# One of the 32 rows of wo in each partition is loaded at the start of the kernel, on ScalarE's DMA queue

## The chip, the cores and the metric

One core of a Trainium2 chip runs the kernel. The metric is the device time in microseconds (us); less is better. The engines are PE (TensorE), DVE (VectorE), ACT (ScalarE), POOL (GpSimd) and SP (SyncE, which here only issues DMAs). DMAs are issued by SP and by ACT, each into a queue of its own, and 16 DMA engines work for both.

## The reference

One decode step. Attention of 16 query heads over 8 cached KV heads of 65,536 positions with 256 elements each, a gated ReLU feed-forward part beside it, and a mix of the two by a scalar gate:

```python
g = sigmoid((x * gate_w).sum(-1, keepdims=True))          # x: [1, 1, 448]
q = (x @ wq).reshape(B, Sq, 16, 256)                       # wq: [448, 4096]
p = softmax(einsum("bhqd,bhkd->bhqk", q, k) / 16)          # k, v: [1, 8, 65536, 256], bf16
a = einsum("bhqk,bhkd->bhqd", p, v).reshape(1, 1, 4096) @ wo   # wo: [4096, 448]
b = (relu(x @ W_gate) * (x @ W_up)) @ W_down               # 448 -> 1792 -> 448
return g * a + (1 - g) * b
```

K and V are 256 MB each and are read once; the weights are some 12 MB. Nearly all that is read is K and V.

## The kernel before, in words

K and V are cut into 32 tiles each of 8 MB (128 partitions of 64 KB), four for each KV head. Three SBUF buffers, `ring0` to `ring2`, take them: K tiles alternate between `ring1` and `ring2`, V tiles use `ring0` until the last four, and the weights use `ring0` while no V tile needs it.

Each K tile is transposed in place by DVE in four instructions (`f_trans`, L529), multiplied by the queries on PE (`f_qk`, L540), reduced to its maximum on DVE (L703) and exponentiated on ACT (L705). V tiles are multiplied on PE (L584). At the end `f_sel` (L557) turns the last head's result into `attnA`, and `f_wo` multiplies it by wo (`proj`, L551), whose 4096 rows lie as 32 rows in each of the 128 partitions. The two halves of the result go through a copy each (L796, L797) and out by one DMA.

The order of the work is written by hand: every operation has an engine and a key, a time that its author planned for it, and each engine executes its operations in the order of their keys. A class `_Plan` works out the semaphore waits. DMAs that SP issues stand in one list (`order`): K tile 0, wq (one large and one small DMA), K tile 1, W_down (`wd`), K tile 2, W_gate and W_up, K tile 3, then K and V tiles by turns, the last V tile in three pieces, and wo in chunks of whole rows (L393):

```python
WO = [(0, 11), (11, 18), (18, 23), (23, 27), (27, 30), (30, 32)]
```

A K tile is issued once the tile two places earlier has been multiplied: K tile 2 waits for the second half of K tile 0's `f_qk`. SP issues in order, so what stands behind such a wait in SP's list waits too.

ACT issues only two DMAs, both at the very start: `x` (one row of 896 bytes, into `P_sb`, L421) and `gate_w` (the same size, into `scr`, L422). What needs them stands early on DVE, ahead of the transposes of K tile 0:

- `x0_` (L478, L479) copies part of x to `xeo`, PE turns x (L485), and DVE spreads it to `xw` (L492, L494), which the projection with wq (`f_q`, L501) needs;
- `z0` to `z9` (L464 to L475, with a step on ACT at L466 and one on PE at L471) work out the gate from x and gate_w, on one partition.

Behind these on DVE come the four transposes of K tile 0 (L529), the transpose of the projected queries (L632, which waits for ACT's copy of them, L630), their spreading to `xm` (L513), and `nselT` (L636). `f_qk` of K tile 0 runs once these are through.

Of the kernel before, what the change touches and what calls it, by code (L numbers as in the profile page):

```python
# [27 lines left out]
class _Plan:  # L28
# [8 lines left out]
    def op(self, eng, key, fn, deps=(), tag=None):  # L37
        eng, cls = {"pv": ("pe", "pv"), "dx": ("dv", "dx"), "ap": ("ac", "ap")}.get(eng, (eng, eng))
        o = _Op(eng, key, fn, deps, tag=tag, cls=cls)
        self.ops.append(o)  # L40
        return o

    def dma(self, eng, key, sem, fn, deps=()):
        if sem not in self.dsem:
            self.dsem[sem] = self.es.enter_context(self.nc.semaphore("d_" + sem))
        o = _Op(eng, key, fn, deps, dma=sem)
        self.ops.append(o)
        return o
# [212 lines left out]
def bass_gated_mix__gqa_block_cached__glu_gated_reglu__decode_kernel(  # L261
# [16 lines left out]
    D = A_x.shape[2]  # L278
# [18 lines left out]
    with es:  # L297
# [4 lines left out]
        P_sb = sb("P_sb", [128, 2048], BF)  # L302
        pcur = [sb("pcur%d" % i, [128, 256], BF) for i in range(2)]
        ptp = sb("ptp", [128, 1024], BF)
        scr = sb("scr", [128, 1024], BF)
# [21 lines left out]
        attnA = sb("attnA", [128, 32], BF)  # L327
# [11 lines left out]
        x_row = P_sb[0:1, 1312:1312 + D]  # L339
        fin_o = P_sb[0:1, 0:D]  # L340
        gw_row = scr[0:1, 0:D]
        xeo = scr[0:1, 448:704]
        qrep = scr[:, 0:512]
        gtmp = ptp[0:1, 0:2 * D].bitcast(F32)

# [25 lines left out]
        op, dma = pl.op, pl.dma  # L371
# [17 lines left out]
        for i, (lo, hi) in enumerate(PIECES):  # L389
            order.append(("vp", i, TILE * (hi - lo) / U))  # L390

        WO = [(0, 11), (11, 18), (18, 23), (23, 27), (27, 30), (30, 32)]
        for i, (lo, hi) in enumerate(WO):  # L393
            order.append(("wo", i, 0.27 * (hi - lo)))
        t = 3.0
        tL, issue = {}, []
# [21 lines left out]
        wo_sb = ring[slot["wo", 0]][:, 0:32 * D].rearrange("p (s n) -> p s n", s=32)  # L418


        d_x = dma("ac", -9, "x", lambda e: e.dma_start(x_row, A_x[0, :, :]))  # L421
        d_gw = dma("ac", -8, "gw", lambda e: e.dma_start(gw_row, gate_w.rearrange("(o d) -> o d", o=1)))  # L422

# [125 lines left out]
        def proj(e, lhsT, rhs, start, stop):  # L549
            for g in range(2):  # L550
                ins = e.matmul(A_ps[32 * g:32 * g + 1, 0:D2], lhsT, rhs[:, g * D2:(g + 1) * D2], start=start, stop=stop,  # L551
                               skip_group_check=True, tile_position=(0, 32 * g))
            return ins
# [7 lines left out]
        l_, qk, smax, aexp, pv, pc, last, first = {}, {}, {}, {}, {}, {}, {}, {}  # L561
# [62 lines left out]
        for kind, i, t in sorted(issue, key=lambda q: q[0] != "wq"):  # L624
# [51 lines left out]
            elif kind == "k":  # L676
                n = i
# [30 lines left out]
                if t_ == NTH - 1:  # L708
# [18 lines left out]
                    for rd in range(2):  # L727
# [10 lines left out]
                        p = op("pe", tt + 0.5, f_ptr, [rsc, g_idb], tag=("ptr", rd))  # L738
# [29 lines left out]
            elif kind in ("v", "vp"):  # L768
                if kind == "v":
                    n, lo, hi = i, 0, U  # L770
# [12 lines left out]
            elif kind == "wo":  # L783
                lo, hi = WO[i]
                l_["wo", i] = dma("sp", t, "wo%d" % i, lambda e, lo=lo, hi=hi: e.dma_start(  # L785
                    wo_sb[:, lo:hi, :], A_wo.rearrange("(p s) n -> p s n", s=32)[:, lo:hi, :]), free(("wo", 0)))

        LAST = last["tn", H - 1]
        aA = op("dx", LAST + 0.3, lambda e: e.tensor_copy(attnA[:], AX_ps), [last["otr", H - 1]])
        for i, (lo, hi) in enumerate(WO):  # L790
            def f_wo(e, lo=lo, hi=hi):
                for s_ in range(lo, hi):
                    ins = proj(e, attnA[:, s_:s_ + 1], wo_sb[:, s_, :], False, s_ == 31)
                return ins
            fin = op("pv", max(LAST + 0.5 + i, tL["wo", i]), f_wo, [l_["wo", i], aA, l_["dn"]])
        f0 = op("dx", T_END, lambda e: e.tensor_copy(fin_o[:, 0:D2], A_ps[0:1, 0:D2]), [fin])  # L796
        f1 = op("ap", T_END, lambda e: e.copy(fin_o[:, D2:D], A_ps[32:33, 0:D2]), [fin])  # L797
        f2 = dma("sp", T_END + 1, "out", lambda e: e.dma_start(out[0, :, :], fin_o), [f0, f1])
# [77 lines left out]
```

## Time and profile before

| | |
|---|---|
| time, median of 3 runs | 1276.04 us (1276.03 to 1276.18) |
| span of the profiled execution, first to last instruction | 1274.3 us |
| bytes read | 549.03 MB, 431 GB/s over the span |
| busy: PE, DVE, ACT, POOL | 29%, 49%, 6%, 0% of the span |
| mean granted clock of TensorE | 0.634 |
| first K tile: issue to landing | 22.1 us |

The page gives no device time for the profiled execution by itself; its span lies 1.7 us under the median of the three runs, which spread over 0.15 us. "L464" is line 464 of the kernel before; in the changed kernel the same lines stand two to four lines further down. In the DMA tables q1 is the queue of the DMAs that SP issues, and q10 that of ACT's: in the whole trace it holds four packets, those of x and gate_w.

### The profile page before, as it was taken

The page shows a single profiled execution, that of the slowest core. Times are in us where ns is not written, and L with a number is a line of the kernel's source. Part 1 is how long each engine was busy: PE and PEld are TensorE (multiplying, and loading weights), DVE is VectorE, ACT ScalarE, POOL GpSimd, SP SyncE. Part 2 cuts the span into 40 slices and gives each one's busy share as a digit, 9 for nine tenths or more (in the row PEclk, how much of TensorE's full clock was granted, in tenths as well). Part 3 has the DMA queues.
Part 4 walks back from the last instruction along what each step waited for, and adds up shares of the span by engine and source line. Part 5 has one row for each costly group of instructions (what it writes and reads, how often), then busy time and mean ns, then how long its engine had stood idle before and what let it go on. Part 6 is the DMA issues. An engine that isn't in the chain of part 4 may idle for free.

```text
span 1274.3 us, 10240 instructions
## 1 busy us (share of the span) xinstructions
PE 365.9 (29%) x4497; PEld 151.4 (12%) x4505; DVE 630.1 (49%) x309; ACT 78.0 (6%) x163; POOL 4.6 (0%) x23
## 2 busy tenths in 40 slices
PE   0534321133320332312233222323302332112525
PEld 0101110011110111101111110111100111001201
DVE  4777655553455633557433565335654355553300
ACT  0001100010000100001000010000000010000100
POOL 1000000000000000000000000000000000000000
PEclk9766665666655666656666656666566666566667
DMA  9999999999999999999999999999999999999998
GB/s 411 430 436 432 426 430 434 432 443 432 430 432 432 434 442 430 430 434 430 438 438 430 430 434 430 440 438 428 430 434 430 444 434 428 430 436 430 442 421 369
DMA packets 11389, 549.13 MB, mean 431 GB/s; under 512 B 1267, under 2 KB 1654, under 8 KB 2294
## 3 DMA queue, kind: packets, MB, share of 16 engines
q1 hardware_dynamic: 11378, 549.03, 99.7%
q8 instruction: 4, 0.07, 0.0%
q14 instruction: 3, 0.02, 0.0%
q10 hardware_dynamic: 4, 0.00, 0.0%
HBM read 549.03 MB, written 0.00 MB: 431 GB/s over the span
## 4 chain that ended last, share of the span: by engine, by line
DMA 81%; PE 16%; DVE 2%; ACT 1%; issue 1%; SPq 0%; ACTq 0%
DMA ring<-in_A_v_cache_dram 74%; PE O L584 13%; DMA ring<-in_A_wo_dram 3%; DMA ring<-in_A_wq_dram 2%; DMA ring<-in_A_k_cache_dram 2%; DVE ring L529 1%; PE ST L540 1%; ACT pcur L591 1%; PE O L501 1%; PE A_ps L551 0%; SPq L785 0%; SPq L776 0%; PE O L653 0%; DVE ring L660 0%; PE A_ps L653 0%
## 5 line engine op out<-in xcount | busy, mean ns | idle before, releaser
L529 DVE STREAM_TRANSPOSE ring<-ring 128x4096 uint32<-128x4096 uint32 x128 | 557.6, 4413 | 196.9 <-DMA ring<-in_A_k_cache_dram 196.9
L584 PE MATMUL O<-ring,pcur 128*4 128x512 bf16 x2048 | 187.3, 545 | 790.4 <-ACT pcur L591 781.9
L703 DVE TENSOR_REDUCE nmb<-ST 128x1 f32<-128x512 f32 x32 | 22.1, 692 | 345.9 <-PE ST L540 345.9
L584 PEld LDWEIGHTS O<-ring,pcur 128*4 128x4 bf16 x2048 | 59.3, 111 | 914.8 <-ACT pcur L591 794.6
L540 PE MATMUL ST<-ring,xcur 128*16 128x512 bf16 x2048 | 136.7, 420 | 44.3 <-DVE ring L529 43.7
L540 PEld LDWEIGHTS ST<-ring,xcur 128*16 128x16 bf16 x2048 | 62.4, 92 | 112.1 <-DVE ring L529 48.6
L705 ACT ACTIVATE P_sb<-ST,nmb 128x512 bf16<-128x512 f32 x32 | 44.6, 1392 | 368.3 <-DVE nmb L703 368.3
L591 ACT COPY pcur<-ptp 128x256 bf16<-128x256 bf16 x32 | 13.2, 415 | 732.6 <-DMA ring<-in_A_v_cache_dram 732.6
L607 DVE TENSOR_SCALAR o_sb<-O,rcm 128x256 bf16<-128x256 f32 x8 | 3.8, 479 | 61.1 <-PE O L584 61.1
L730 DVE TENSOR_TENSOR P_sb<-P_sb,hs 128x1024 bf16<-128x1024 bf16 x16 | 18.9, 1222 | 8.1 <-ACT hs L724 8.1
L735 PE MATMUL PT<-identb,P_sb 128*128 128x128 bf16 x128 | 14.5, 282 | 17.6 <-DVE P_sb L730 17.3
L501 PE MATMUL O<-ring,P_sb 128*128 128x512 bf16 x28 | 8.5, 477 | 17.3 <-DMA ring<-in_A_wq_dram 17.3
L735 PEld LDWEIGHTS PT<-identb,P_sb 128*128 128x128 bf16 x128 | 10.7, 127 | 19.9 <-DVE P_sb L730 19.9
L744 ACT COPY ptp<-PT 128x256 bf16<-128x256 bf16 x32 | 10.3, 375 | 23.0 <-PE PT L735 23.0
L705 ACT ACTIVATION_READ_ACCUMULATOR P_sb<-ST,nmb 128x1 f32 x32 | 8.3, 258 | 0.0
L501 PEld LDWEIGHTS O<-ring,P_sb 128*128 128x128 bf16 x28 | 3.2, 117 | 22.2 <-issue 20.5
L551 PE MATMUL A_ps<-ring,attnA 128*1 128x224 bf16 x64 | 5.3, 322 | 1.1 <-DMA ring<-in_A_wo_dram 1.0
L719 PE MATMUL M_ps<-identf,hs 128*2 128x128 f32 x8 | 2.3, 283 | 10.0 <-DVE hs L717 10.0
L756 DVE RECIPROCAL rc<-M_ps 128x2 f32<-128x2 f32 x8 | 1.4, 171 | 7.5 <-PE M_ps L755 7.5
L755 PE MATMUL M_ps<-hs,ones_f 128*128 128x2 f32 x16 | 4.5, 352 | 0.0
L722 PE MATMUL M_ps<-mx,nselT 2*128 2x1 f32 x16 | 3.2, 268 | 3.0 <-DVE mx L721 3.0
L755 PEld LDWEIGHTS M_ps<-hs,ones_f 128*128 128x128 f32 x16 | 4.0, 311 | 0.0
(93 smaller groups left out, 68.6 us busy)
## 6 DMA issues: line engine op xcount, KB each, us to landing
ring<-in_A_v_cache_dram SPq DMA_DIRECT2D x1, 4096.0 KB, 22.1
ring<-in_A_wq_dram SPq DMA_DIRECT2D x1, 3072.0 KB, 28.9
ring<-in_A_v_cache_dram SPq DMA_DIRECT2D x1, 3072.0 KB, 28.8
ring<-in_B_W_down_dram SPq DMA_DIRECT2D x1, 1568.0 KB, 53.0
ring<-in_B_W_gate_dram SPq DMA_DIRECT2D x1, 1344.0 KB, 26.3
ring<-in_B_W_up_dram SPq DMA_DIRECT2D x1, 1344.0 KB, 29.2
ring<-in_A_wo_dram SPq DMA_DIRECT2D x1, 1232.0 KB, 33.0
ring<-in_A_v_cache_dram SPq DMA_DIRECT2D x1, 1024.0 KB, 30.7
```

The source lines that it names most:

```text
L501: ins = e.matmul(QN_ps, xw3[:, kt, 31 - m:159 - m], rhs, start=(kt == 0 and m == 0), stop=(kt == R3 and m == J // 4 - 1))
L529: return lambda e: e.transpose(v, v)
L540: ins = e.matmul(bank[32 * w:32 * w + 16, :], xcur[:, x0:x0 + 16], ktv[sl][:, u0:u0 + 16, c, :, r_], start=(b == 0 and c == 0 and r_ == 0) ...
L551: ins = e.matmul(A_ps[32 * g:32 * g + 1, 0:D2], lhsT, rhs[:, g * D2:(g + 1) * D2], start=start, stop=stop, skip_group_check=True, tile_pos ...
L584: ins = e.matmul(OP[32 * g:32 * g + 4, :], pcur[a % 2][:, 4 * k:4 * k + 4], ring[sl][:, k * 512:(k + 1) * 512], start=False, stop=False, s ...
L591: pc[n] = op("ap", max(tp - 5, last["tev", h] - 0.5), lambda e: e.copy(pcur[a % 2][:].rearrange("p (k i) -> p k i", i=4), ptp[:].rearrange ...
L703: smax[n] = op("dv", sx, lambda e, n=n, t_=t_: e.tensor_reduce(NM[:, t_:t_ + 1], ST[n % 2][:], AX.X, ALU.max, negate=True), [qk[n, 1], las ...
L705: aexp[n] = op("ac", sx + 1, lambda e, n=n, t_=t_: e.activation(P_sb[:, t_:2048:4], ST[n % 2][:], ACTF.Exp, bias=NM[:, t_:t_ + 1], scale=1 ...
L730: rsc = op("dv", tt, lambda e, pb=pb: e.tensor_tensor(pb, pb, X[:, 12:16].unsqueeze(1).to_broadcast([128, 256, 4]), ALU.mult), [h7, aexp[n]])
L735: ins = e.transpose(PT[rd][:, s * 128:(s + 1) * 128], P_sb[:, (rd * 8 + s) * 128:(rd * 8 + s + 1) * 128], identb[:, :])
L744: ins = e.copy(dst, src)
L755: l3 = mop("pe", T + 19, lambda e: e.matmul(LS_ps, ones_f[:, :], X[:, 6:8], start=True, stop=True), [l2, c_one], tag="l3")
```

## The change

wo's row 31 in each partition no longer comes with the last chunk. It is a DMA of its own, `d_wl`, with 128 rows of 896 bytes (0.11 MB), into a free part of `scr`, and ACT issues it as its first, ahead of x and gate_w. The last chunk of wo has one row in each partition instead of two, and ends with row 30. The product with row 31 is taken first of all 32, and waits for `d_wl` too. `xeo` moves from `scr` to `P_sb`, since `wo_l` takes its place.

```diff
-        xeo = scr[0:1, 448:704]
+        xeo = P_sb[0:1, 1776:2032]
+        wo_l = scr[:, 576:576 + D]
...
-        WO = [(0, 11), (11, 18), (18, 23), (23, 27), (27, 30), (30, 32)]
+        WO = [(0, 11), (11, 18), (18, 23), (23, 27), (27, 30), (30, 31)]
...
+        d_wl = dma("ac", -10, "wl", lambda e: e.dma_start(wo_l[:], A_wo.rearrange("(p s) n -> p s n", s=32)[:, 31, :]))
         d_x = dma("ac", -9, "x", lambda e: e.dma_start(x_row, A_x[0, :, :]))
         d_gw = dma("ac", -8, "gw", lambda e: e.dma_start(gw_row, gate_w.rearrange("(o d) -> o d", o=1)))
...
             def f_wo(e, lo=lo, hi=hi):
+                if lo == 0:
+                    proj(e, attnA[:, 31:32], wo_l[:], False, False)
                 for s_ in range(lo, hi):
-                    ins = proj(e, attnA[:, s_:s_ + 1], wo_sb[:, s_, :], False, s_ == 31)
+                    ins = proj(e, attnA[:, s_:s_ + 1], wo_sb[:, s_, :], False, s_ == 30)
                 return ins
-            fin = op("pv", max(LAST + 0.5 + i, tL["wo", i]), f_wo, [l_["wo", i], aA, l_["dn"]])
+            fin = op("pv", max(LAST + 0.5 + i, tL["wo", i]), f_wo, [l_["wo", i], aA, l_["dn"], d_wl])
```

The start of ACT's program before (`P_sb` from `in_A_x` is x, `scr` from `in_gate_w` is gate_w):

```order
L836 UNCONDITIONAL_BRANCH
L421 DMA P_sb<-in_A_x_dram 1x448
L422 DMA scr<-in_gate_w_dram 1x448
L466 ACT_TABLE_LOAD
L466 ACTIVATE gz<-gz 1x1
L630 CAST ptp<-O 128x512
L634 COPY xcur<-xm 128x136
```

The same place in the changed kernel:

```order
L840 UNCONDITIONAL_BRANCH
L422 DMA scr<-in_A_wo_dram 128x448
L423 DMA P_sb<-in_A_x_dram 1x448
L424 DMA scr<-in_gate_w_dram 1x448
L468 ACT_TABLE_LOAD
L468 ACTIVATE gz<-gz 1x1
L632 CAST ptp<-O 128x512
L636 COPY xcur<-xm 128x136
```

The new DMA stands ahead of both others; nothing else on ACT moves, and DVE's order stays as it was.

The end of PE's program before, with the semaphores that a row waits for (`d_wo1` to `d_wo5` are the landings of the chunks of wo):

```order
L551 MATMUL A_ps<-ring,attnA 1x224 [waits s_dx,d_wo0]
L551 MATMUL A_ps<-ring,attnA 1x224 x21
L551 MATMUL A_ps<-ring,attnA 1x224 [waits d_wo1]
L551 MATMUL A_ps<-ring,attnA 1x224 x13
L551 MATMUL A_ps<-ring,attnA 1x224 [waits d_wo2]
L551 MATMUL A_ps<-ring,attnA 1x224 x9
L551 MATMUL A_ps<-ring,attnA 1x224 [waits d_wo3]
L551 MATMUL A_ps<-ring,attnA 1x224 x7
L551 MATMUL A_ps<-ring,attnA 1x224 [waits d_wo4]
L551 MATMUL A_ps<-ring,attnA 1x224 x5
L551 MATMUL A_ps<-ring,attnA 1x224 [waits d_wo5]
L551 MATMUL A_ps<-ring,attnA 1x224 x3
```

And in the changed kernel, from the second matmul with row 31 (the first stands one row ahead and waits for `d_wl`, `s_dx` and `d_wo0`):

```order
L553 MATMUL A_ps<-scr,attnA 1x224
L553 MATMUL A_ps<-ring,attnA 1x224 x22
L553 MATMUL A_ps<-ring,attnA 1x224 [waits d_wo1]
L553 MATMUL A_ps<-ring,attnA 1x224 x13
L553 MATMUL A_ps<-ring,attnA 1x224 [waits d_wo2]
L553 MATMUL A_ps<-ring,attnA 1x224 x9
L553 MATMUL A_ps<-ring,attnA 1x224 [waits d_wo3]
L553 MATMUL A_ps<-ring,attnA 1x224 x7
L553 MATMUL A_ps<-ring,attnA 1x224 [waits d_wo4]
L553 MATMUL A_ps<-ring,attnA 1x224 x5
L553 MATMUL A_ps<-ring,attnA 1x224 [waits d_wo5]
L553 MATMUL A_ps<-ring,attnA 1x224
```

The two matmuls with row 31 move from behind the last wait to the first group, and behind the last wait two are left of four.

## The prediction

> **What bounds the kernel now.** I read the page first, for the share of the DMA engines, then the chain that ended last at both ends of the program, and then the start of ACT and DVE in the timeline, since that is where the change puts its new transfer. The page's DMA rows:
>
> ```profile
> DMA  9999999999999999999999999999999999999998
> DMA packets 11389, 549.13 MB, mean 431 GB/s; under 512 B 1267, under 2 KB 1654, under 8 KB 2294
> q1 hardware_dynamic: 11378, 549.03, 99.7%
> q10 hardware_dynamic: 4, 0.00, 0.0%
> ```
>
> The 16 DMA engines are busy in every slice, and SP's queue alone fills 99.7% of them. So a stretch in which they stand idle is added to the time, and bytes that only change their place take nothing off it. The reader should keep one figure from here: 431 GB/s over 16 engines is 26.9 GB/s for one, so a row of 64 KB, as each partition of a K tile has, takes one engine 65,536 / 26.9e3 = 2.43 us. A K tile is 128 rows, eight for each engine. The chain at the start and at the end:
>
> ```profile
> 1.66 29.70 DMA ring<-in_A_wq_dram
> 31.49 8.51 PE O L501 x28
> 50.70 24.64 DMA ring<-in_A_k_cache_dram
> ...
> 1236.40 35.84 DMA ring<-in_A_wo_dram
> 1272.24 0.04 issue
> 1272.28 0.38 PE A_ps L551 x4
> 1272.66 0.02 issue
> 1272.68 0.38 DVE P_sb L796
> ```
>
> K tile 2 is issued at 50.70, when K tile 0 is through, and lands at 75.34. At the end the last chunk of wo lands at 1272.24, four matmuls take 0.38, and a copy and the store follow. Everything between is transfers.
>
> **The change part by part.** At the end two things shrink. The last chunk has 0.11 MB less, which at 431 GB/s is 0.27 us of transfer, but these bytes are read at the start instead: whether that saves anything depends on whether they find idle engines there, so this term lies between -0.27 and 0, and below 0 on the bad side too by a little, since 128 rows of 1,792 bytes become 256 of 896 with an end packet more. I put it at -0.2. Behind the last wait two matmuls of four are left: at 0.38 / 4 apiece that is -0.19, but the pipeline's last result takes its time whatever stands ahead of it, so between -0.19 and 0; I take -0.1. The two matmuls moved to the first group lie beside the wait for the next chunks, and the wait for `d_wl` there comes over a millisecond after its issue: nothing. `xeo` in another tile is the same three small instructions on DVE: nothing. The tail is worth about -0.3, between -0.46 and +0.1.
>
> At the start ACT now issues 128 rows ahead of x and gate_w, while SP issues K tile 0. How the two queues shared the engines before is seen best in the packets of ACT's queue, q10. It holds four in all: two for each of its two DMAs, which I read as the row and the packet that signals its end (the table counts packets by size, and one in each pair is under 512 bytes). The DMA view over six stretches, 1.5 to 1.7, 1.7 to 7.3, 7.3 to 7.4 (both queues), 7.4 to 9.7 and 9.7 to 9.8 us:
>
> ```profile
> DMA packets 2, 0.00 MB, mean 4 GB/s; under 512 B 1, under 2 KB 2, under 8 KB 2
> q10 hardware_dynamic: 2, 0.00, 1.9%
> ...
> q1 hardware_dynamic: 33, 2.16, 101.4%
> ...
> q1 hardware_dynamic: 3, 0.20, 453.6%
> q10 hardware_dynamic: 1, 0.00, 2.6%
> ...
> q1 hardware_dynamic: 12, 0.79, 78.9%
> ...
> q1 hardware_dynamic: 4, 0.26, 604.8%
> q10 hardware_dynamic: 1, 0.00, 0.6%
> ```
>
> x goes through at 1.5 to 1.7, just before K tile 0's first row starts. gate_w does not: it waits until 7.3, while 33 K rows start on the 16 engines (two on each, and a third on one), and then its end packet waits until 9.7, one K row of 2.43 us more. So an engine that has K rows waiting serves ACT's queue by turns: one K row, one packet of ACT, one K row. The issues and the first users of these two DMAs, from the timelines of ACT's and SP's queue and of DVE:
>
> ```profile
> 0.72 0.52 ACTq L421 DMA_DIRECT2D P_sb<-in_A_x_dram  x1
> 1.27 0.21 ACTq L422 DMA_DIRECT2D scr<-in_gate_w_dram  x1
> 0.72 0.42 SPq L680 DMA_DIRECT2D ring<-in_A_k_cache_dram  x1
> 4.92 0.18 DVE L478 COPY scr<-P_sb 1x64 bf16<-1x64 bf16 x1
> 6.04 0.18 DVE L494 COPY P_sb<-xT 128x4 bf16<-128x4 bf16 x1
> 10.15 0.61 DVE L464 TENSOR_TENSOR ptp<-P_sb,scr 1x448 f32<-1x448 bf16 x1 [3.93 <-DMA scr<-in_gate_w_dram]
> 13.57 0.58 PE L471 MATMUL M_ps<-gz,ones_f 1*128 1x2 f32 x2 [8.01 <-DVE gz L470]
> 14.38 0.23 DVE L475 TENSOR_SCALAR mg<-emat,gb 128x4 f32<-128x4 bf16 x1
> 22.81 17.42 DVE L529 STREAM_TRANSPOSE ring<-ring 128x4096 uint32<-128x4096 uint32 x4 [8.20 <-DMA ring<-in_A_k_cache_dram]
> 40.70 0.45 DVE L632 STREAM_TRANSPOSE scr<-ptp 128x256 uint32<-128x256 uint32 x1 [0.47 <-ACT ptp L630]
> ```
>
> gate_w, issued at 1.27, reached DVE at 10.15. DVE needed 14.61 - 10.15 = 4.46 us for the gate, and then stood idle for 8.20 us until K tile 0 had landed. That idle time is the cover under which gate_w's wait is free now.
>
> With the change, ACT's queue has on the engine that serves x and gate_w eight rows and an end packet of the new DMA, then two packets of x, then two of gate_w: 13 where there were 4. K tile 0 and the new DMA are issued at the same moment (0.72 both, in place of x). I take it that one packet gets ahead of K's first row, as x's did, and the rest go by turns. Eight go behind the eight rows of K tile 0, which then ends at 22.81 - 0.4 + 0.27 = 22.7 (0.4 is what DVE took from gate_w's end packet at 9.7 to 9.8 until L464 at 10.15; 0.27 is the new rows' own time). Four are left, and these take turns with wq's rows. The DMA view of 21.75 to 29.0 us gives their length:
>
> ```profile
> DMA packets 144, 3.15 MB, mean 434 GB/s; under 512 B 16, under 2 KB 16, under 8 KB 16
> ```
>
> That is eight rows and an end packet for each engine in 7.25 us, 0.91 for a row. gate_w ends at T = 22.7 + 4 x 0.91 = 26.3; x two turns earlier, at 24.5.
>
> From T on the steps are those of before. DVE starts the gate at T + 0.4, and the transposes of K tile 0, which stand behind it on DVE, at T + 0.4 + 4.46 = 31.2 instead of 22.81: 8.4 late. Of this 0.47 is absorbed, where L632 waited for ACT. So K tile 2 is issued at 50.70 + 8.4 - 0.47 = 58.6. What else waits has cover: the projection with wq, at 31.49, needs x spread, which is done 1.3 us after x lands (4.92 to 6.22), at 25.8; and the gate's matmul, which stands ahead of it on PE, ends 4.0 us after L464 starts, at 30.7.
>
> Is a late K tile 2 paid? SP's queue has wq, K tile 1 and W_down behind K tile 0. The DMA issues of the page and, last, of the stretch of 0 to 1 us, with their sizes and times to landing, below SP's issue of W_down:
>
> ```profile
> 2.71 0.53 SPq L675 DMA_DIRECT2D ring<-in_B_W_down_dram  x1
> ...
> ring<-in_A_wq_dram SPq DMA_DIRECT2D x1, 3072.0 KB, 28.9
> ring<-in_B_W_down_dram SPq DMA_DIRECT2D x1, 1568.0 KB, 53.0
> ring<-in_A_wq_dram SPq DMA_DIRECT2D x1, 512.0 KB, 29.7
> ...
> ring<-in_A_k_cache_dram SPq DMA_DIRECT2D x1, 22.1
> ```
>
> Two K tiles of 8.39 MB, wq's 3.67 and W_down's 1.61 are 22.1 MB, 51.2 us at 431 GB/s from 1.7 on: the queue is dry at 53, and W_down, issued at 2.71, lands by 55.7 with all that stands ahead of it. The first K tile, issued into an idle queue, took 22.1 us to land.
>
> So K tile 2, issued at 58.6 into a queue run dry, lands at 80.7 instead of 75.34, +5.4. In general, T decides from 75.34 - 22.1 = 53.24 on, that is from T = 20.9, and each microsecond more costs one. Nothing behind it gives that back: the engines stay full afterwards, so the whole stream of K and V shifts, and DVE and PE, which wait for transfers in most of the span, shift along. With the tail, 5.4 - 0.3 = 5.1 us: 1276.04 + 5.1 = 1281.1 (1279.4 in the span's terms).
>
> The bounds: with two packets ahead of K's first row T is 25.4, with three 24.5, +3.2 in all; with none, and the first turn missed as gate_w's was, T is 28.1, +6.9. That gives 1279.2 to 1283.0.
>
> **The rivals.** First, **the new rows are through before K tile 0 begins**. Nothing then waits for them, and the tail's gain is all there is: -0.5 to 0, so 1275.5 to 1276.0. For it: x did get through ahead of K. Against it: x was a single row, and now eight rows and an end packet are due on each of 16 engines, and K's rows come right behind x (none before 1.7, 33 in the stretch after it). It decides where T stays under 20.9, which takes six of the eight rows ahead of K. Chance 0.20.
>
> Second, **an engine takes ACT's rows in bulk when their turn comes**. gate_w would then land about where it does now, near 10, or a K row or two later, under DVE's cover of 8.20 us: again 1275.5 to 1276.1. For it: no queue in this trace had more than one row waiting beside K's, so the trace doesn't exclude it. Against it: gate_w's own two packets did not go together, but had a K row between them. Chance 0.11. The Trainium skill, "DMA: Bandwidth & Descriptors", section "Queues, rings and completion order", has such a rule: each DMA engine goes round the queues that have work, and drains a whole packet, typically 9 to 17 descriptors, before it turns to the next. By that rule all 13 would need one or two turns and this rival would hold. The trace's q10 rows speak against it, as far as two packets can.
>
> Third, **half of the new rows get ahead**, four to five: T is 22.7 to 23.6, +1.4 to +2.4 with the tail, 1277.4 to 1278.4, and with half a turn more 1278.9. The same rows speak for it and against it as for the first. Chance 0.06.
>
> A gain above the tail's has no source in the profile, since the engines have no idle time to fill but the first 1.7 us: 0.01.
>
> **How the numbers follow.** The forecast has 0.62, and 1281.1 is its time. Its own range is 1279.2 to 1283.0. The first two rivals hold 0.31 between them, so a range that holds 8 in 10 has to reach down to 1275.5; upwards it ends at 1283.0. About 0.2% (2.55 us) is what a measurement of this kernel can tell from no change. Slower by more than that: the forecast and a third of the third rival, 0.64. Within it: the first two rivals and two thirds of the third, 0.35. Faster: 0.01.
>
> **What would show it.** Right: DVE's L466 (L464 before) starts near 26 to 27; the transposes of K tile 0 start near 31 and not 22.81; K tile 2 is issued near 58.6; the DMA view shows idle engines between 54 and 59. The last PE group has x2 and ends about 0.1 us sooner behind its landing. Wrong: gate_w reaches DVE before 18, K tile 0's transposes start at 22.8 to 23.2, and no idle stretch shows; then either q10's packets all lie before K's first row (the first rival) or they come in one bunch between two K rows (the second).

## The result, and the profile after

The changed kernel took 1278.91 us (median of 7 runs, 1278.28 to 1281.31) against 1276.04 before (7 runs, 1275.9 to 1276.97): 1.0025 times as long, 95% interval 1.0015 to 1.0036. It is slower, by 2.9 us. The profiled execution has a span of 1277.1 us, 2.8 more than before.

The page of the changed kernel, its DMA rows:

```profile
DMA packets 11533, 549.13 MB, mean 430 GB/s; under 512 B 1283, under 2 KB 1798, under 8 KB 2438
...
q1 hardware_dynamic: 11378, 548.92, 99.5%
q10 hardware_dynamic: 148, 0.12, 0.1%
```

The same bytes are read, and 0.11 MB of them have moved from SP's queue q1 to ACT's q10. But q1 has 99.5% of a longer span instead of 99.7%: 0.005 x 1277.1 against 0.003 x 1274.3 leaves the engines 2.6 us more without a packet of SP (the shares are rounded, so to within about a microsecond). The timelines of ACT's queue, DVE and SP's queue say where:

```profile
0.71 0.40 ACTq L422 DMA_DIRECT2D scr<-in_A_wo_dram  x1
1.15 0.53 ACTq L423 DMA_DIRECT2D P_sb<-in_A_x_dram  x1
1.71 0.24 ACTq L424 DMA_DIRECT2D scr<-in_gate_w_dram  x1
22.75 0.20 DVE L480 COPY P_sb<-P_sb 1x64 bf16<-1x64 bf16 x1 [17.74 <-DMA P_sb<-in_A_x_dram]
24.02 0.60 DVE L466 TENSOR_TENSOR ptp<-P_sb,scr 1x448 f32<-1x448 bf16 x1
28.39 17.42 DVE L531 STREAM_TRANSPOSE ring<-ring 128x4096 uint32<-128x4096 uint32 x4
45.73 0.40 DVE L634 STREAM_TRANSPOSE scr<-ptp 128x256 uint32<-128x256 uint32 x1
54.95 0.33 SPq L682 DMA_DIRECT2D ring<-in_A_k_cache_dram  x1
```

x, which was there by 4.92 before, lets DVE go on at 22.75, and the 17.74 us in brackets are its wait for that DMA. The gate starts at 24.02 instead of 10.15. The row of the transposes has no bracket any more: they no longer wait for K tile 0 but for what stands ahead of them on DVE, and start 5.6 us late. K tile 2 is issued 4.25 us late. The view by stretches of 1 us shows the engines without work before it; its last two columns are the busy share of the DMA engines and GB/s:

```profile
53.00:54.00 1.00, 1.00 (x20) 0.46 (x16) 0.00 (x0) 0.00 (x0) 0.00 (x0) 0.90 0.71 289
54.00:55.00 1.00, 0.89 (x16) 0.22 (x8) 0.05 (x1) 0.00 (x0) 0.00 (x0) 1.00 0.06 25
```

What the engines moved from 1 to 120 us, in the DMA view, first of the kernel before:

```profile
DMA packets 1745, 51.33 MB, mean 431 GB/s; under 512 B 191, under 2 KB 449, under 8 KB 577
```

and of the changed kernel:

```profile
DMA packets 1854, 50.00 MB, mean 420 GB/s; under 512 B 194, under 2 KB 580, under 8 KB 708
```

1.33 MB less, which is 3.1 us at 431 GB/s. The loss is there by 120 us, within the first tenth of the program.

How the queues took turns is seen in the DMA view over 0 to 4.6, 4.6 to 7.1, 14.6 to 17.1 and 17.1 to 18.3 us (q1 is SP's, q10 ACT's; the first number counts packets):

```profile
q1 hardware_dynamic: 16, 1.05, 60.8%
q10 hardware_dynamic: 48, 0.04, 9.2%
...
q1 hardware_dynamic: 16, 1.05, 96.9%
q10 hardware_dynamic: 16, 0.01, 1.6%
...
q1 hardware_dynamic: 16, 1.05, 96.7%
q10 hardware_dynamic: 16, 0.01, 1.6%
...
q1 hardware_dynamic: 16, 1.05, 201.5%
q10 hardware_dynamic: 16, 0.00, 0.8%
```

With 16 engines, 48 packets by 4.6 us are three rows for each, around the first row of K. After that 16 rows of K start in each stretch of a K row's time, and 16 packets of ACT's queue. The fourth pair is the new DMA's 16 end packets (0.00 MB). x and gate_w come behind them.

### The profile page after: what moved, and what is told of

It is laid out like the page before. It is cut to its first block, busy times and chain, and to the rows that moved or that the text cites. A ratio compares the mean times of both kernels' runs of the same rounds, so it can differ in the third digit from the quotient of the medians.

```text
span 1277.1 us, 10249 instructions
## 1 busy us (share of the span) xinstructions
PE 358.2 (28%) x4505; PEld 148.8 (12%) x4505; DVE 629.9 (49%) x309; ACT 78.0 (6%) x163; POOL 4.6 (0%) x23
## 3 DMA queue, kind: packets, MB, share of 16 engines
q1 hardware_dynamic: 11378, 548.92, 99.5%
## 4 chain that ended last, share of the span: by engine, by line
DMA 79%; PE 15%; DVE 3%; issue 1%; ACT 1%; SPq 0%; ACTq 0%
DMA ring<-in_A_v_cache_dram 74%; PE O L586 13%; DVE ring L531 3%; DMA ring<-in_A_wo_dram 3%; DMA ring<-in_A_wq_dram 2%; PE ST L542 1%; ACT pcur L593 1%; PE O L503 1%; PE A_ps L553 1%; SPq L778 0%; DVE nmb L705 0%; DVE ring L662 0%; PE A_ps L655 0%; PE O L655 0%; ACTq L166 0%
## 5 line engine op out<-in xcount | busy, mean ns | idle before, releaser
L586 PE MATMUL O<-ring,pcur 128*4 128x512 bf16 x2048 | 179.1, 526 | 796.3 <-ACT pcur L593 787.2
L705 DVE TENSOR_REDUCE nmb<-ST 128x1 f32<-128x512 f32 x32 | 22.1, 692 | 339.7 <-PE ST L542 339.7
L487 PE MATMUL M_ps<-one_t,P_sb 1*128 1x1 bf16 x5 | 0.3, 160 | 23.2 <-DVE P_sb L481 23.2
L573 PE MATMUL O<-zer,identb 128*128 128x512 bf16 x8 | 4.7, 587 | 0.0
```

Of the source, the lines that this page charges most:

```text
L573: last["zo", h] = op("pv", key, lambda e: e.matmul(OP[:], identb[:, :], zer[:, 0:1].to_broadcast([128, 512]), start=True, stop=True, skip_ ...
L586: ins = e.matmul(OP[32 * g:32 * g + 4, :], pcur[a % 2][:, 4 * k:4 * k + 4], ring[sl][:, k * 512:(k + 1) * 512], start=False, stop=False, s ...
L705: smax[n] = op("dv", sx, lambda e, n=n, t_=t_: e.tensor_reduce(NM[:, t_:t_ + 1], ST[n % 2][:], AX.X, ALU.max, negate=True), [qk[n, 1], las ...
```

## The experiments

The expectations speak of a theory W and its rivals. W: x and gate_w wait behind the new rows in ACT's queue, one packet for each row of K; DVE, which works in order, starts K tile 0's transposes late, and K tile 2 is issued too late to find the engines busy. The rivals put the loss into the small rows themselves, into their bytes, or into the end of the program.

**The new rows behind x and gate_w.**

```diff
-        d_wl = dma("ac", -10, "wl", ...
+        d_wl = dma("ac", -7, "wl", ...
```

> The changed kernel with one edit: ACT issues the new rows of wo behind x and gate_w instead of ahead of them. Theory W (the whole loss is x and gate_w waiting behind the new rows in ACT's queue, which holds up DVE, the transposes of K tile 0 and so the issue of K tile 2): gate_w lands near 10 again, the transposes start at 22.8 to 23.1, K tile 2 is issued at 50.7 to 51.2, no idle engines near 54; 1276.0 to 1276.4, the 0.25 above the kernel before being 0.11 MB that now stand ahead of all of K and V. The prediction's term for the tail (-0.3) would make it 1275.7. Rival C (the loss is the 128 small rows in between K tile 0's, or the wait for them on PE at the end): still 1278.5 to 1279.0.

Measured: 1275.84 us (11 runs, 1275.6 to 1276.29) against 1275.83 (15 runs), 1.0 times, interval 0.9991 to 1.0009. In the timeline of DVE and of SP's queue:

```profile
10.11 0.61 DVE L466 TENSOR_TENSOR ptp<-P_sb,scr 1x448 f32<-1x448 bf16 x1 [3.89 <-DMA scr<-in_gate_w_dram]
23.28 17.43 DVE L531 STREAM_TRANSPOSE ring<-ring 128x4096 uint32<-128x4096 uint32 x4 [8.70 <-DMA ring<-in_A_k_cache_dram]
50.79 0.33 SPq L682 DMA_DIRECT2D ring<-in_A_k_cache_dram  x1
```

gate_w lands as before, the transposes wait for K tile 0 again, and K tile 2 is issued as early as before. The 128 rows still went through between K tile 0's rows and wq's first ones, and the end of the program is that of the changed kernel. So neither the rows nor the end cost anything that can be seen: the loss is their place ahead of x and gate_w. It shows, too, that the rest of the change gains nothing that can be seen: the medians agree within 0.01, where the expectation had put this kernel 0.25 above, though the interval alone would allow 1.1 us either way.

**The start alone.** In the kernel before, the same rows are issued first, as a spare copy that only the products with wo at the end wait for.

```diff
+        d_wl = dma("ac", -10, "wl", ...[:, 31, :]))      # WO unchanged
...
-            fin = op("pv", ..., [l_["wo", i], aA, l_["dn"]])
+            fin = op("pv", ..., [l_["wo", i], aA, l_["dn"], d_wl])
```

> The kernel before with one edit: ACT issues the same 128 rows first of all, but as a spare copy; wo's chunks stay as they were and all 32 rows come with them, so the end of the program is untouched and 0.11 MB is read twice. Theory W: x lands at 20 to 25, K tile 2 is issued at 54 to 57, 1278.5 to 1281.5, as the changed kernel or up to 0.3 above it. Rival (the loss comes from the end, where row 31 now stands first on PE and the last chunk is short): within 0.3 of 1276.0.

Measured: 1280.97 us (5 runs, 1279.79 to 1281.52), 1.004 times (1.0027 to 1.0054). DVE's transposes start at 28.52 and K tile 2 is issued at 55.83. The start alone makes the loss.

**Twice the bytes in as many rows.** The spare copy has rows of 1,792 bytes.

```diff
+        d_wl = dma("ac", -10, "wl", ...(ring[0][:, 24576:24576 + 2 * D], ...[:, 30:32, :]...
```

> As e2_spare, but rows of 1,792 bytes: as many rows for each engine (eight), twice the bytes, 0.23 MB, into a part of a ring buffer that is free until V tile 0. Theory W by turns (an engine gives ACT's queue a turn between K rows, and what counts is how many descriptors stand ahead of x): x lands where it does in e2_spare, within one K row (2.4 us); the time is e2_spare's plus 0.25 for the bytes. Rival, by bytes: the wait grows with the bytes and x lands 10 us or more later than before, at 30 or beyond.

Measured: 1281.56 us (5 runs, 1279.2 to 1281.9), 1.0044 times (1.0031 to 1.0058); its first user on DVE got x at 23.00, 0.12 later than in the run with half the bytes (22.88), and gate_w 0.55 later. Bytes don't set the wait: what is later fits the count of rows, since two rows for each engine got ahead of K here and three there.

**As many bytes in twice as many rows.** 256 rows of 448 bytes.

```diff
+        d_wl = dma("ac", -10, "wl", ...(wo_l.rearrange("p (s n) -> p s n", s=2), ...[:, 15:32:16, 0:D // 2]))
```

> As e2_spare, but 256 rows of 448 bytes: the same bytes in twice as many rows, 16 for each engine. Theory W by turns: about eight more packets stand ahead of x; those that find K tile 0 gone take turns with wq's rows of 0.91 us. gate_w lands at 26 to 28, K tile 2 is issued at 58 to 60, 1282 to 1284. Rival, by bytes: as e2_spare within 0.5.

Measured: 1286.57 us (5 runs, 1285.6 to 1286.89), 1.0081 times (1.0068 to 1.0095). x let DVE go on at 30.16 and the transposes started at 35.80. The count of rows sets the wait. The size was missed by some 3 us. In this profile ACT's queue got no packet through before 7.1 us: none had got ahead of K, and the turn between K's first and second rows was missed as well.

**The changed kernel again**, unedited, twice.

> The changed kernel once more, unedited, to see how its time spreads and to stand beside the next kernels on one chip. Theory W: x's and gate_w's packets fall into turns between K rows of 2.4 us, so a turn more or less is some 2.4 us: times near 1278.5 and near 1281, few between. Rival (one fixed cost): a spread as narrow as that of the kernel before, 0.5 us.

> The changed kernel once more for its profile. At 1278.3 to 1279.1: three rows ahead of K tile 0 and gate_w at 23.3, as in the two profiles before. At 1280.8 to 1281.4: none or one ahead, gate_w at 25.2 to 27, K tile 2 issued at 57 to 59.

Measured: 1280.86 us (5 runs, 1278.44 to 1281.15), 1.0035 times (1.0022 to 1.0049), and 1277.93 in the single run. Over all 13 runs eight lie between 1277.9 and 1279.1 and five between 1280.8 and 1281.4: two levels, 2.4 us or so apart. All three profiles fell on the lower one; each shows 48 packets of q10 by 4.6 us and gate_w's last packet at 23.2 to 23.4. The upper level wasn't caught in a trace, and the next run stands in for it. The traced run is the first of each series. In four of the five series that begin with eight rows for each engine (this one, the spare copy, twice the bytes, the gate moved) it is also the fastest, in the last two by 1.8 and 2.4 us. So the traces may show the lower level more often than the runs had it; why isn't known.

**K tile 0's rows surely first.** ACT waits for a short memset of DVE before it issues the new rows, with x and gate_w still behind them.

```diff
-        d_wl = dma("ac", -10, "wl", ...[:, 31, :]))
+        d_wl = dma("ac", -0.09, "wl", ...[:, 31, :]), [c_xe])
...                                       # d_x and d_gw: -0.08 and -0.07, behind d_wl
```

> The changed kernel, but ACT waits for one early memset of DVE (done at about 1.05 us) before it issues the new rows, so that K tile 0's rows are in the engines' queues first. In the profiles so far 16 packets of ACT's queue, one for each engine, go through in each K row's time, and three of the eight rows got ahead of K tile 0 in the two profiles of the changed kernel. Theory W with one packet per turn: none gets ahead now; 13 packets take the nine turns of K tile 0 (eight rows and the end packet, to 22.4) and four of wq's of 0.91 us: gate_w lands at 26 to 27, transposes start at 31 to 32, K tile 2 is issued at 57.5 to 59; all runs near the upper of the two levels, 1281 to 1282.5, none near 1278.5. Rival (the two levels have nothing to do with which queue comes first): 1278.4 to 1281.3 as before.

Measured: 1281.48 us (4 runs, 1281.32 to 1282.26), 1.0042 times (1.0025 to 1.0059). The timelines of ACT's queue, DVE and SP's queue:

```profile
1.06 0.42 ACTq L427 DMA_DIRECT2D scr<-in_A_wo_dram  x1
27.14 0.61 DVE L467 TENSOR_TENSOR ptp<-P_sb,scr 1x448 f32<-1x448 bf16 x1 [0.50 <-DMA scr<-in_gate_w_dram]
31.52 17.41 DVE L532 STREAM_TRANSPOSE ring<-ring 128x4096 uint32<-128x4096 uint32 x4
58.17 0.33 SPq L683 DMA_DIRECT2D ring<-in_A_k_cache_dram  x1
```

An issue 0.35 us later puts every run on the upper level. The steps lie where the prediction had put them for one packet ahead (gate at 26.7, transposes at 31.2, K tile 2 at 58.6), though here none was ahead and ACT's first packet came only at 7.3, behind K's second row. That the unedited kernel's upper runs are those in which no row gets ahead fits, but is argued and not traced.

**ACT's rows surely first.** SP waits for a memset of DVE before it issues K tile 0. For that its first DMA, which was issued ahead of the engines' programs, moves into SP's own.

```diff
-                kd = dma("sp", t, ..., free(("k", n)))
+        hold0 = c_xw
...
+                kd = dma("sp", t, ..., free(("k", n)) + ([hold0] if n == 0 else []))
...
-        pl.emit("sp", progs["sp"][:1], nc.sync, seen_sp)
+        pl.emit("sp", progs["sp"][:0], nc.sync, seen_sp)
```

> The changed kernel, but SP waits for an early memset of DVE (done at about 1.5 us) before it issues K tile 0, so that ACT's rows are in the engines' queues first. Theory W: all or nearly all of the new rows are through before K tile 0 begins, x too; gate_w lands at 8 to 15, the transposes start when K tile 0 lands, K tile 2 is issued without idle engines before it; what is left is the later start of all transfers, 0.6 to 1.0 us: 1276.5 to 1277.0. Rival (the new rows cost the same wherever they lie): 1279 or more.

Measured: 1276.73 us (10 runs, 1276.31 to 1278.47), 1.0007 times (0.9998 to 1.0017). The DMA view of its first 4.6 us:

```profile
q10 hardware_dynamic: 146, 0.12, 10.5%
```

And the timelines of SP's queue and of DVE:

```profile
1.48 0.42 SPq L683 DMA_DIRECT2D ring<-in_A_k_cache_dram  x1
8.52 0.61 DVE L466 TENSOR_TENSOR ptp<-P_sb,scr 1x448 f32<-1x448 bf16 x1 [2.31 <-DMA scr<-in_gate_w_dram]
23.54 17.43 DVE L531 STREAM_TRANSPOSE ring<-ring 128x4096 uint32<-128x4096 uint32 x4 [10.55 <-DMA ring<-in_A_k_cache_dram]
```

146 of 148 packets are through before the second row of K, and the wait is gone. What is left is about the 0.76 us by which K tile 0 is issued later, 1.48 instead of 0.72. One of the ten runs, 1278.47, lies 1.3 above all others and was not traced. This is the first rival made to happen, and its price.

**Half the rows.** The spare copy of 64 rows, four for each engine.

```diff
+        d_wl = dma("ac", -10, "wl", ...(wo_l[0:64], ...[0:64, 31, :]))
```

> As e2_spare, but half the transfer: 64 rows of 896 bytes, four for each engine, issued first by ACT as a spare copy. Theory W with its threshold (a late K tile 2 costs nothing until it is issued at about 53, that is, until gate_w lands at about 21): three K rows fewer are waited for, gate_w lands at 16 to 20 and DVE is through with the gate before or just after K tile 0 lands: 1275.8 to 1276.4. Rival (a cost in proportion to the rows): half of e2_spare's 5, 1278 to 1278.5.

Measured: 1278.13 us (11 runs, 1277.26 to 1279.08), 1.0016 times (1.0007 to 1.0025). The expectation for W missed, and the time lies in the range of the rival, a cost in proportion to the rows. But the wait is not half: DVE takes up gate_w at 23.40, against 24.15 with all the rows and 10.15 with none. In the stretch of 0 to 4.6 us no packet of q10 stands at all: of these rows none got ahead of K, where three of eight had. Four rows, an end packet, x's two and gate_w's two are nine packets, and nine turns are all of K tile 0. By number of packets behind K's first row it had only one fewer than the changed kernel (nine against ten), so the run doesn't test the threshold it was made for.

**The step on DVE.** In the changed kernel the gate's last steps move behind the first and second of the four transposes.

```diff
-        z3 = op("dx", 1.3, ...       # z4 1.4, z5 1.5, z6 1.6 (PE), z7 1.7, z9 1.9
+        z3 = op("dx", 23, ...        # z4 23.1, z5 23.2, z6 23.3 (PE), z7 27, z9 27.1
```

> The changed kernel with the new rows still first, but the gate's last steps moved on DVE from ahead of the four transposes of K tile 0 to between them, where their inputs are ready: only the spreading of x and the gate's first two steps stay ahead. Theory W, the step on DVE: the transposes start 3.1 us sooner behind gate_w's landing, near 25.3 for a landing at 23.3, are through 2.2 us sooner, and K tile 2 is issued at 52.5 to 53.5: 1276.0 to 1277.0, in a run with one turn more up to 1279. Rival (what counts is the landing of x on PE and the projection with wq, not DVE's order): unchanged, 1278.5 to 1281.5.

> e5_gate once more for its profile, since the profiled run of it took 1275.70 and the other ten 1278.1 to 1279.6. Theory W with the order of the queues: in a run at the upper level no new row gets ahead of K tile 0, gate_w lands at 26 to 27 instead of 23.4, and K tile 2 is issued at 54 to 56 instead of 51.8. Rival (PE's clock makes the two levels): gate_w lands at 23.4 again, and PE's steps between 32 and 56 are 2 us longer.

Measured: 1278.5 us (11 runs, 1275.7 to 1279.6), 1.0022 times (1.0013 to 1.0031), and 1276.59 in the single run. The two profiles are of the runs of 1275.70 and 1276.59. From the first, DVE's and SP's timeline:

```profile
24.10 0.61 DVE L466 TENSOR_TENSOR ptp<-P_sb,scr 1x448 f32<-1x448 bf16 x1
25.27 4.42 DVE L531 STREAM_TRANSPOSE ring<-ring 128x4096 uint32<-128x4096 uint32 x1
51.82 0.33 SPq L682 DMA_DIRECT2D ring<-in_A_k_cache_dram  x1
```

With the gate started at 24.10, as in the changed kernel, the transposes start 3.1 us sooner, K tile 2 is issued at 51.82, and the loss is gone in that run. So DVE's order is part of the mechanism. The median doesn't say so by itself: 1278.5 is within W's allowance for one turn more, and at the edge of the rival's range. In the second profile gate_w landed at the same time but PE took 6.22 us for K tile 0 instead of 4.95, and K tile 2 was issued at 52.95; the span is 0.9 longer. So PE's speed goes into the time once K tile 2 is late. The ten other runs, 1278.1 to 1279.6, were not traced, since the second profile, which was to show one of them, is of a faster run. They lie some 2.5 us below the changed kernel's upper level, as the 2.4 us by which DVE is through with the transposes sooner would have it if they belong there. Why this kernel fell there so often is open, and so is the rival that PE's speed makes the levels; over all the profiles PE's time for K tile 0 differs by 1.5 us, less than the 2.4 between the levels.

**The delay of DVE alone.** The kernel before, with two memsets on DVE ahead of K tile 0's transposes and no DMA touched.

```diff
+                if n == 0:
...
+                    l_["hold"] = op("dx", tk - 0.1, f_hold, [kd])      # two memsets in a free part of ring0
```

> The kernel before, its DMAs and their order untouched, with two memsets of some 2.2 us each on DVE between the landing of K tile 0 and its transposes. Theory W, the last steps by themselves (late transposes, late issue of K tile 2, idle engines): transposes start at 27.0 to 27.5, K tile 2 is issued at 53.9 to 55.0, the engines stand idle 1.5 to 2.5 us, 1277.5 to 1278.8. Rival (a delay of DVE early on is made up for later, and the loss of the changed kernel comes from the transfers): 1276.0 to 1276.4.

Measured: 1278.31 us (11 runs, 1277.47 to 1280.06), 1.0019 times (1.001 to 1.0028). DVE's and SP's timeline:

```profile
23.09 1.98 DVE L685 MEMSET ring<- 128x2304 uint32 x1 [8.22 <-DMA ring<-in_A_k_cache_dram]
27.39 17.36 DVE L529 STREAM_TRANSPOSE ring<-ring 128x4096 uint32<-128x4096 uint32 x4
53.78 0.33 SPq L680 DMA_DIRECT2D ring<-in_A_k_cache_dram  x1
```

A delay of DVE alone, with x and gate_w on time, costs 2.4 us. It is not made up for later.

The profiles together, ordered by the issue of K tile 2:

| profile | transposes of K tile 0 start | K tile 2 issued | span |
|---|---|---|---|
| before | 22.81 | 50.70 | 1274.3 |
| rows behind x and gate_w | 23.28 | 50.79 | 1274.4 |
| ACT's rows surely first | 23.54 | 51.63 | 1274.6 |
| gate moved, first profile | 25.27 | 51.82 | 1273.9 |
| gate moved, second profile | 25.14 | 52.95 | 1274.8 |
| delay of DVE alone | 27.39 | 53.78 | 1276.1 |
| half the rows | 27.78 | 54.06 | 1276.2 |
| changed kernel, third profile | 28.43 | 54.34 | 1276.1 |
| changed kernel, second profile | 28.31 | 54.73 | 1276.6 |
| changed kernel | 28.39 | 54.95 | 1277.1 |
| twice the bytes | 29.08 | 55.22 | 1277.4 |
| spare copy | 28.52 | 55.83 | 1277.9 |
| K tile 0's rows surely first | 31.52 | 58.17 | 1280.4 |
| twice the rows | 35.80 | 63.16 | 1285.1 |

Up to about 52 the span doesn't depend on K tile 2's issue. Beyond it each microsecond costs one: 54.95 - 52.1 = 2.8, and 58.17 - 52.1 = 6.1, as measured (2.8 and 6.1). The 52.1 is read off these two rows; the others beyond it follow within 0.5 us. No variant beat the kernel before. The best form of the change, with the new rows behind x and gate_w, equals it.

## Why the prediction was right, and where its sizes were off

The direction and the mechanism were right at each step that the runs could see: ACT's queue gets one packet between two rows of K; x and gate_w come last in it; DVE's order passes that on to K tile 0's transposes; K tile 2 is issued after SP's queue has run dry; the idle time is not given back. Undoing the first step alone (rows behind x and gate_w) takes the whole loss away, and making the last steps alone (delay of DVE) makes a loss.

The size was 5.1 us, and the measured one 2.9 at the median. 1278.91 lies 0.3 below the forecast's own range of 1279.2 to 1283.0; the stated range reached lower only for the first two rivals, which did not come about, so that it holds the result is partly luck. In the first profile of the changed kernel four terms were off: the transposes of K tile 0 start at 28.39 instead of 31.2 (-2.8, from the rows that got ahead), K tile 2 is issued 26.6 us behind that and not 27.4 (-0.9, mostly PE, which took 5.70 us for K tile 0 where it took 6.45 before), the threshold lies earlier (+1.1), and the tail gains nothing (+0.3). Together they take 5.1 to 2.8.

**How many rows get ahead of K tile 0.** I took one, from x's single packet; in the profiles of the changed kernel it was three. For three my bounds gave T = 24.5 and 1279.2. gate_w's last packet came at 23.3, about a turn of wq's rows sooner, since K tile 0's own end packet is a turn as well: it offers nine turns and not eight. x's end packet and gate_w's row both went at 22.4, within 0.02 us. With none ahead, as was forced in one run, the median is 1281.48, and the prediction's 1281.1, for one ahead, lies beside it. That is luck in part: for none ahead and the first turn missed, as in that run, the prediction's sum gave T = 28.1 and 1283.0, and gate_w's last packet came at 26.8. The forecast's time fits the kernel's upper level; it didn't see that there are two, and that the kernel's own range reaches from one to the other.

**The tail.** I put it at -0.3, and with the rows behind x and gate_w, where nothing else is left of the change, the medians differ by 0.01. The timeline of DVE at the end shows what became of it. Before (the copy to `attnA`, then the last copy):

```profile
1266.23 0.19 DVE L789 CAST attnA<-A_ps 128x32 bf16<-128x32 f32 x1 [0.46 <-PE A_ps L557]
1272.68 0.38 DVE L796 CAST P_sb<-A_ps 1x224 bf16<-1x224 f32 x1 [6.26 <-PE A_ps L551]
```

With the new rows behind x and gate_w:

```profile
1266.66 0.19 DVE L791 CAST attnA<-A_ps 128x32 bf16<-128x32 f32 x1 [0.46 <-PE A_ps L559]
1272.81 0.38 DVE L800 CAST P_sb<-A_ps 1x224 bf16<-1x224 f32 x1 [5.96 <-PE A_ps L553]
```

From the first row to the second is 6.45 us before and 6.15 after: the end is indeed 0.3 shorter, by 0.3 to 0.4 in each of five profiles in which PE still waits for a later chunk. But `attnA` comes 0.43 later here. The bytes give a reason: 0.11 MB read at the start stands ahead of all of K and V, an estimated 0.27 us at 431 GB/s. One trace doesn't show it, since this one is of the slowest of the eleven runs, and with the gate moved `attnA` came at 1266.13 in the first profile. The equal medians are what shows that nothing is left. The prediction had said itself that bytes which only change their place take nothing off, and had put these 0.27 us into K tile 0's landing; still it booked 0.2 for them at the end. The -0.1 for two matmuls of four behind the last wait was not what counted either: with the rows behind x and gate_w the last wait has eight matmuls behind it, so it is for the last chunk but one. And in two of the changed kernel's three profiles the chain that ended last goes through all 64 matmuls with wo, without a wait for a later chunk, here in the first:

```profile
1269.40 6.04 PE A_ps L553 x64
```

There PE was the bound at the end and not the last chunk's landing, and only 0.1 of the gain is left (6.36 from row to row).

The threshold lies a little earlier than the prediction had it: K tile 2 costs from an issue at about 52.1, not 53.24. I had taken K tile 0's 22.1 us to landing for a tile issued into an idle queue, and reckoned by landings. Landing means the last of 16 engines, and they end at different times: in the kernel before, K tile 2's last rows end between 73.1 and 74.9 us, and in the changed one between 75.8 and 76.9. The last engine is 2.0 us later, the 16 are 2.6 us later in the mean, and the span is 2.8 longer. So the landing understates the loss; that this makes up all of the 1.1 us is argued, not shown.

Of the rivals, the first (all rows ahead of K) needs K tile 0 issued 0.76 us later. The second, rows in bulk, did not happen: the trace shows 16 packets of ACT's queue, one for each engine, in each row of K. The Trainium skill ("DMA: Bandwidth & Descriptors", section "Queues, rings and completion order") says that an engine drains a whole packet, typically 9 to 17 descriptors, of a queue before it turns to the next. These traces don't agree with it: one row, and not 9 to 17, went in each turn. The third (some rows ahead) is what happened at the lower level, with three rows and not four to five.

## What to carry to other kernels

In these runs, what counted ahead of a small load on a second DMA queue was not the bytes but the number of rows, and each of them waited for one row of the other queue, here 64 KB and 2.4 us. Small loads that something waits for go first, and large or patient ones behind them; in this case that one exchange was worth all that the change lost. In this program, whose transfers never pause, moving bytes to the start gained nothing, since they then stand ahead of everything, and a pause near the start was paid in full at the end.

## What the runs showed of the hardware that was not expected

- Which of two DMAs issued within 0.01 us of each other comes first isn't the same for every shape: of eight rows of 896 bytes for each engine three got ahead of K's first row in each profile, of eight of 1,792 bytes two, of four of 896 or sixteen of 448 none. In those last two ACT's issue started at 0.72 us, as SP's did, and took 0.55 and 0.63 us; in the others it started at 0.71 and took 0.40. So whether the shape or this order decides isn't shown. An issue 0.35 us later loses every place, and one 0.77 us earlier wins nearly all.
- The packet that ends a DMA takes a turn of its own, as the prediction had read it, and on the busy queue it gives one: with K tile 0's own the other queue gets nine turns for eight rows.
- PE took between 4.95 and 6.49 us for the same 64 matmuls of K tile 0 in these profiles. In the kernel before, this is hidden; in the changed one it goes into the time, and is a part of why its runs spread over 3 us where those before spread over 1. The larger part are the two levels.
